# Reordering the start of an attention-plus-FFN kernel on Trainium2: first transposes of the second batch, last transposes and first values of the first

## The chip, the cores and the metric

The kernel runs on one core of one Trainium2 chip. The metric is device time in microseconds (us). Each kernel is run several times; a median and the range of its runs are quoted.

## The reference, cut to what matters

```python
scores = (1 / sqrt(64)) * q @ k.transpose(0, 1, 3, 2)   # q, k, v: 8 batches, 12 heads, 448 tokens, 64
attn   = maximum(scores, 0.0) ** 2 / 448
x      = (attn @ v), heads side by side                 # 3584 tokens x 768
g, val = x @ w_gate, x @ w_val                          # 768 -> 1536
out    = (gelu(g) * val) @ w_out                        # 1536 -> 768
```

Inputs and output are float32; the kernel computes in bf16.

## The kernel before

The host side of the kernel makes a list of pieces of work with a wished time each, sorts it, splits TensorE's work into a list for the lower and one for the upper half of the array (by `tile_position` matmuls use 64x64 quarters), and then plays the lists through a small model that decides the final order of instructions of each engine. So a change of a wished time moves instructions on all engines. Inside a batch, "transposes" turn the loaded q and k, 21 "score units" each give TensorE matmuls, one relu on ScalarE and one square on VectorE, "values" multiply the squares by v, and "gate pieces" (with w_gate or w_val) and "output pieces" (with w_out) are the FFN. The first batch has nothing to run beside its attention, so TensorE fills holes with dummy matmuls (18 with 512 columns each between 5 and 31 us in before).

```python
    def fill(t0, t1):                       # dummy matmuls in a hole of TensorE, early in the kernel only
        ...
        n = int((t1 - t0 - 0.15) / 0.22)
        if t1 > FILL or n < 1:
            return
        t = new_bank(None)
        for _ in range(n):
            nc.tensor.matmul(t[:, :], warm[:, 0:128], warm[:, :], start=True, stop=True)
...
    PLACE5 = -7.0                           # wished time of the first batch's last values
    def add_gate_value(at, b, fc, g):
        ...
        if (b, fc) == (0, 0):               # the first gate slice stands around those last values
            at = [PLACE5 - 0.5 + 0.1 * g] * 3 + [PLACE5 + 0.1] + [0.01 * g] * 2
        then(at, GS, *ops, done)
...
    for m in range(NM):                     # third batch: the last loads of the starting list
        for i in range(2):
            load_qk(2, i, 4 * m, 4 * m + 4)
    load_v(2, 0, H)
...
    LO1 = 2 * G + 2.2                       # where the second batch's attention may begin
    for b in range(B):
        if b == 0:
            lo, hi = -60.0, -12.0
        elif b == 1:
            lo, hi = LO1, starts[1] - LEAD
        ...
        step = (hi - lo) / NU
        if b < EARLY:
            for m in range(NM):
                for rs in ((0,), (1,)) if b == 0 else ((0, 1),):
                    x = (1.5 * step if rs == (1,) else -3.0) if b == 0 else -5.0 if m else -2.0
                    work.append((lo + SC * m * step + x, 1, add_transposes, (b, m, rs)))
        for pr in range(NPAIR):
            u = SC * (pr // 2) + (VC - 1, SC - 1)[pr % 2]
            x = lo + u * step + max(4.5, (3.2 if b == 0 else 2.5) * step)
            work.append((PLACE5 if (b, pr) == (0, NPAIR - 1) else x, 2, add_values, (b, pr)))
        for u in range(NU):
            work.append((lo + u * step, 3, add_scores, (b, u)))
    work.sort(key=lambda w: w[:2])
...
    def emit_warm_up():                     # the first matmuls of the program: 20 dummies
        t = new_bank(None)
        for _ in range(10):
            for j in range(2):
                nc.tensor.matmul(t[HALF[j], :], warm[:, HALF[j]], warm[:, :],
                                 start=True, stop=True, tile_position=(0, P * j))
```

## Time and profile before

| | before |
|---|---|
| time, median of the first 3 runs (range) | 428.75 us (428.64 to 429.78) |
| span of the profiled run, granted clock | 427.4 us, 0.999 |
| TensorE busy | 421.1 us, 99% |
| ScalarE, VectorE busy | 52%, 50% |
| useful TensorE work (counted as for the leads below) from 5.4 us (first transpose) to 31 us | 12.4 of 25.6 us of the array's capacity |

How to read it: TensorE is the bound, and its busy share hides two things. In the first 31 us busy time contains dummy matmuls (6.0 us from 5 to 31 us); that is where the change works. And a TensorE that stands still for some tenths of a us hardly shows, because the trace gives a 448-column matmul a length of some 0.35 us, though the next one follows 0.189 us after its start.

### The profile page before, as it was taken

The page shows a single profiled execution, that of the slowest core. Times are in us where ns is not written, and L with a number is a line of the kernel's source. Part 1 is how long each engine was busy: PE and PEld are TensorE (multiplying, and loading weights), DVE is VectorE, ACT ScalarE, POOL GpSimd, SP SyncE. Part 2 cuts the span into 40 slices and gives each one's busy share as a digit, 9 for nine tenths or more (in the row PEclk, how much of TensorE's full clock was granted, in tenths as well). Part 3 has the DMA queues.
Part 4 walks back from the last instruction along what each step waited for, and adds up shares of the span by engine and source line. Part 5 has one row for each costly group of instructions (what it writes and reads, how often), then busy time and mean ns, then how long its engine had stood idle before and what let it go on. Part 6 is the DMA issues. An engine that isn't in the chain of part 4 may idle for free.

```text
span 427.4 us, 19594 instructions
## 1 busy us (share of the span) xinstructions
PE 421.1 (99%) x9090; PEld 359.7 (84%) x9093; DVE 213.1 (50%) x347; ACT 223.5 (52%) x320; POOL 71.5 (17%) x116
## 2 busy tenths in 40 slices
PE   8999999999999999999999999999999999999996
PEld 3556768889998889889999988979999988977895
DVE  2865766367653665346643566445743555212201
ACT  4946674366655555556455565555546555322220
POOL 8655320012200131012300123011310000000000
PEclk9999999999999999999999999999999999999999
DMA  7999999978984399545965379635984100120034
GB/s 103 191 199 198 201 208 195 161 104 110 119 130 88 46 112 119 118 83 84 134 116 114 47 91 147 133 63 57 136 141 98 38 4 3 44 72 3 2 77 114
DMA packets 75217, 44.91 MB, mean 105 GB/s; under 512 B 36096, under 2 KB 71680, under 8 KB 75136
## 3 DMA queue, kind: packets, MB, share of 16 engines
q0 software_dynamic: 37088, 24.39, 42.6%
q1 hardware_dynamic: 37888, 19.08, 24.8%
q8 instruction: 71, 1.16, 1.2%
q10 hardware_dynamic: 160, 0.20, 0.1%
q14 instruction: 10, 0.08, 0.1%
HBM read 48.76 MB, written 11.01 MB: 140 GB/s over the span
## 4 chain that ended last, share of the span: by engine, by line
PE 98%; ACT 0%; issue 0%; DVE 0%; ACTq 0%
PE ff L159 86%; PE sp L159 8%; PE ff L304 1%; PE ff L699 1%; PE sp L342 1%; PE ff L342 1%; ACT rl L389 0%; DVE osb L555 0%; DVE warm L145 0%; DVE table L148 0%; ACTq L389 0%
## 5 line engine op out<-in xcount | busy, mean ns | idle before, releaser
L159 PE MATMUL ff<-xT,wg 64*64 64x448 bf16 x2304 | 218.2, 349 | 0.0
L159 PE MATMUL ff<-xT,wv 64*64 64x448 bf16 x2304 | 216.7, 349 | 0.1
L389 ACT ACTIVATE rl<-sp 128x896 bf16<-128x896 f32 x168 | 152.3, 918 | 94.3 <-PE sp L159 77.6
L159 PE MATMUL ff<-wo,uT 64*64 64x384 bf16 (+1 forms) x2736 | 151.4, 320 | 0.0
L159 PEld LDWEIGHTS <-wg 64*64 64x64 bf16 x2304 | 126.9, 107 | 17.3 <-issue 0.9
L159 PEld LDWEIGHTS <-wv 64*64 64x64 bf16 x2304 | 126.8, 107 | 17.3 <-issue 2.1
L395 DVE TENSOR_TENSOR attnT<-rl 128x896 bf16<-128x896 bf16 x168 | 103.8, 623 | 69.1 <-ACT rl L389 68.2
L159 PEld LDWEIGHTS <-uT 64*64 64x64 bf16 x2736 | 128.7, 107 | 3.9
L159 PE MATMUL sp<-qkT 64*64 64x448 bf16 (+1 forms) x768 | 108.3, 328 | 0.5 <-ACT rl L389 0.4
L503 DVE TENSOR_TENSOR uT<-gel,ff 128x448 bf16<-128x448 bf16 x96 | 59.5, 620 | 79.2 <-PE ff L159 68.4
L159 PE MATMUL ff<-attnT,v 64*64 64x448 bf16 (+1 forms) x768 | 86.2, 326 | 0.1
L498 ACT ACTIVATE gel<-ff 128x448 bf16<-128x448 f32 x96 | 52.1, 543 | 55.5 <-PE ff L159 54.7
L159 PEld LDWEIGHTS <-qkT 64*64 64x64 bf16 x768 | 44.1, 106 | 9.8 <-issue 4.2
L159 PEld LDWEIGHTS <-v 64*64 64x64 bf16 x768 | 46.7, 107 | 5.4 <-issue 1.3
L555 ACT COPY osb<-ff 128x384 f32<-128x384 f32 x54 | 25.7, 476 | 46.0 <-PE ff L159 43.3
L448 DVE TENSOR_SCALAR xT<-ff 128x448 bf16<-128x448 f32 x48 | 29.9, 623 | 31.5 <-PE ff L159 31.4
L211 POOL DMA_DIRECT2D qk<-in_q_dram x25 | 15.5, 622 | 128.7 <-DVE uT L503 121.6
L224 POOL DMA_DIRECT2D v<-in_v_dram x44 | 27.3, 627 | 41.6 <-DVE uT L503 32.0
L211 POOL DMA_DIRECT2D qk<-in_k_dram x25 | 15.4, 615 | 64.1 <-DVE uT L503 55.7
L258 DVE COPY qkr<-qk 128x1792 bf16<-128x1792 bf16 x18 | 19.3, 1077 | 0.0
L555 DVE COPY osb<-ff 128x192 f32<-128x192 f32 (+1 forms) x3 | 1.2, 421 | 18.3 <-PE ff L159 18.3
L342 PEld LDWEIGHTS <-qk 128*64 128x64 bf16 x168 | 5.5, 115 | 3.6 <-issue 3.2
(23 smaller groups left out, 44.3 us busy)
## 6 DMA issues: line engine op xcount, KB each, us to landing
out_dram<-osb SPq DMA_DIRECT2D x54, 192.0 KB, 2.9
v<-in_v_dram POOLq DMA_DIRECT2D x42, 128.0 KB, 4.0
qk<-in_q_dram POOLq DMA_DIRECT2D x23, 224.0 KB, 4.4
qk<-in_k_dram POOLq DMA_DIRECT2D x23, 224.0 KB, 4.7
wg<-in_moe_w_gate_dram POOLq DMA_DIRECT2D x6, 384.0 KB, 10.2
wv<-in_moe_w_val_dram POOLq DMA_DIRECT2D x6, 384.0 KB, 11.1
wo<-in_moe_w_out_dram POOLq DMA_DIRECT2D x4, 576.0 KB, 15.4
v<-in_v_dram POOLq DMA_DIRECT2D x2, 384.0 KB, 11.2
```

Source lines behind the costliest of these rows:

```text
L159: return nc.tensor.matmul(o, lhsT, rhs, start=start, stop=stop, tile_position=(P * row, P * col))
L211: op = load(4 * (h1 - h0) * S * D, lambda: nc.gpsimd.dma_start(tile_of().rearrange("p (h x) -> p h x", h=H)[:, h0:h1, :], src[b, h0:h1].re ...
L224: return nc.gpsimd.dma_start(v16[b][HALF[i], h0:h1, :, :], v[b, h0:h1].rearrange("h (p c) d -> p h c d", c=SC)[:, :, c0:c0 + VC, :])
L258: nc.vector.tensor_copy(qkr[b][:, m], qk16[b].rearrange("p (h c d) -> p c h d", c=SC, d=D)[:, :, 4 * m:4 * m + 4])
L304: nc.tensor.matmul(t[:, :], warm[:, 0:128], warm[:, :], start=True, stop=True)
L342: nc.tensor.transpose(t[HALF[j], c, :], src[:, 2 * (2 * m + r) + j, c, :], ident[:, :], tile_position=(0, P * j))
L389: nc.scalar.activation(rl[:, :, :], box[0][:, :, 0:S], AF.Relu)
L395: nc.vector.tensor_tensor(a[:, :, :], box[1][:, :, :], box[1][:, :, :], op=ALU.mult)
L448: nc.vector.tensor_scalar_mul(xT[b][:, pr, :], box[0][:, 0:S], scalar1=out_scale)
L498: nc.scalar.activation(gel[b, fc][:, :], box[0][:, 0:S], AF.Gelu)
L503: u_op[b, fc].ins = nc.vector.tensor_tensor(uT[b][:, fc, :], gel.pop((b, fc))[:, :], box[0][:, 0:S], op=ALU.mult).ins
L555: (nc.vector.tensor_copy if last else nc.scalar.copy)(osb[t][:, cols], box[0][:, 0:N])
```

## The change

Its intent is to use the half-empty start. The second batch's first transposes run while the first batch's last values are copied (instead of dummies and idle time), the last group's transposes of the first batch come one unit sooner, the first values come 1.5 units later, and the second batch's window starts 2.5 us sooner.

```diff
         if (b, fc) == (0, 0):
-            at = [PLACE5 - 0.5 + 0.1 * g] * 3 + [PLACE5 + 0.1] + [0.01 * g] * 2
+            at = [PLACE5 - 0.5 + 0.1 * g] * 3 + [0.01 * g] * 3
...
-    LO1 = 2 * G + 2.2
+    LO1 = 2.0
...
-                    x = (1.5 * step if rs == (1,) else -3.0) if b == 0 else -5.0 if m else -2.0
-                    work.append((lo + SC * m * step + x, 1, add_transposes, (b, m, rs)))
+                    x = -5.0 if m else -2.0
+                    if b == 0:
+                        x = (1.5 * step if rs == (1,) else -3.0) - step * (m == NM - 1)
+                    t_at = lo + SC * m * step + x
+                    if (b, m) == (1, 0):
+                        t_at = PLACE5 + 0.05
+                    work.append((t_at, 1, add_transposes, (b, m, rs)))
...
-            x = lo + u * step + max(4.5, (3.2 if b == 0 else 2.5) * step)
+            x = lo + u * step + max(4.5, (3.2 + 1.5 * (pr == 0) if b == 0 else 2.5) * step)
```

## The prediction

> **What bounds the kernel now.** First the page, for the busy shares and the chain:
>
> ```profile
> PE 421.1 (99%) x9090; PEld 359.7 (84%) x9093; DVE 213.1 (50%) x347; ACT 223.5 (52%) x320; POOL 71.5 (17%) x116
> PE 98%; ACT 0%; issue 0%; DVE 0%; ACTq 0%
> ```
>
> TensorE is 99% busy and is 98% of the chain, so nearly nothing off it can pay. But busy is not full. Matmuls here use one 64x64 quarter of the array, four run at once, and a 448-column one holds its quarter for 189 ns (starts in the trace follow at 0.189 us). Four per 0.189 us are 21.2 a microsecond. So next I counted matmuls per stretch (busy us, then count in brackets):
>
> ```profile
> 15.00:25.00 10.00, 9.36 (x146) 1.00 1.41 198
> 25.00:31.00 6.00, 5.89 (x92) 1.00 1.38 199
> 31.00:41.00 10.00, 10.00 (x218) 1.00 1.41 198
> 380.00:390.00 10.00, 10.00 (x220) 1.00 0.04 10
> ```
>
> From 31 us on the array is close to full (21.8 a us, some of them shorter pieces). Before that it runs at 15, and part of these are not work, as the groups from 5 to 31 us show:
>
> ```profile
> L304 PE MATMUL ff<-warm 128*128 128x512 bf16 x18 | 6.0, 386 | 0.3 <-issue 0.3
> ```
>
> Those are fillers[...].[...] useful work from 5.4 to 31 us is about 13 of 25.6 us. So there are some 12 us of slack at the start and almost none later; the change works in just this slack. What ends the waits there is ScalarE's list:
>
> ```profile
> 7.57 5.78 ACT L389 ACTIVATE rl<-sp 128x896 bf16<-128x896 f32 x7 [5.34 <-PE sp L159]
> 13.70 5.01 ACT L389 ACTIVATE rl<-sp 128x896 bf16<-128x896 f32 x6 [0.36 <-PE sp L159]
> 19.10 6.89 ACT L389 ACTIVATE rl<-sp 128x896 bf16<-128x896 f32 x8 [0.38 <-PE ff L159]
> ```
>
> The first batch's 21 score units are 21 relus, starting 0.797 to 0.813 us apart when nothing holds them. The first starts at 7.57, the last at 25.05: 17.48 us against 20 x 0.805 = 16.1, so about 1.4 us of it are waits for TensorE (0.47 before the 8th, 0.51 before the 14th, 0.4 in small ones). After the last relu come its square, the last values, the copies of the values (the rows of VectorE at 26.97 and 27.98) and the first gate matmuls:
>
> ```profile
> 26.93 1.00 PE L159 MATMUL ff<-attnT,v 64*64 64x448 bf16 x6
> 27.75 0.38 PE L159 MATMUL ff<-xT,wg 64*64 64x448 bf16 x2
> 28.44 0.39 PE L304 MATMUL ff<-warm 128*128 128x512 bf16 x1
> 28.76 0.38 PE L159 MATMUL ff<-xT,wg 64*64 64x448 bf16 x2
> 29.82 0.58 PE L342 MATMUL sp<-ident,qk 128*64 128x128 bf16 x14
> 30.33 0.38 PE L159 MATMUL ff<-xT,wg 64*64 64x448 bf16 x2
> 30.64 0.58 PE L342 MATMUL sp<-ident,qk 128*64 128x128 bf16 x14
> ```
>
> The last values issue at 27.37 and 27.56; their copy ends at 28.60; the gate matmul that reads it starts at 28.76. The second batch's first two transpose blocks come only at 29.82 and 30.64, one gate piece between them.
>
> [...] transposes (128x64 tiles) start 0.28 us after the preceding 64x64 piece instead of 0.189, and the next 64x64 piece starts 0.512 us after a block whose 14 matmuls issue in 0.37. A lone block thus costs about 0.8 us.[...]
>
> **The change, part by part.** No work is added or removed; TensorE's rows differ by fillers alone. I took the new order of each engine and the semaphore counts in the built program, and walked it by hand with durations from the trace: relu 0.80 from the last and 0.43 after its scores start, score after a freed buffer 0.05, transposes to copy 0.62, copies and squares 0.54 apart, fillers 0.31 plus 0.21 for each further one.
>
> (a) First values later. The 8th unit's scores now come before the first values, but four fillers instead of one stand ahead of them: 12.30 + 0.31 + 3 x 0.21 = 13.26, relu at 13.69, where it was at 13.70. No gain here.
>
> (b) Last group's transposes a unit sooner. Following the relus: 11th 16.29 (was 16.19, its transpose copy now sits behind a square), 13th 17.99 (17.78), 14th 18.80 (19.10), 16th 20.45 (20.71), 18th 22.08 (22.64), 21st 24.48 (25.05). The wait before the 14th goes, because the transposes no longer stand in front of its scores and the copy is ready in time for the 15th. VectorE is tighter in between (three more copies queue near 20 us) but ends its 21st square at 26.12 (26.645). From there the order is as before, so values, first gate pieces and last copies move by 0.57 us: the last values piece from 27.56 to 26.99. Gain 0.57.
>
> (c) The transposes while the last values are copied. Call the last values piece t. Before: next gate pieces with a 0.31 + 0.32 us hole for the copy, two lone blocks, and the first gate piece of the third slice at t + 5.71. After: block at t + 0.28, second 0.37 later with no switch between, gate at t + 0.655 + 0.512 = t + 1.17; the copy has landed by then (t + 1.04). New wait: the second batch's first scores now come three gate pieces on, and both transpose copies wait for the second block, so they are ready at t + 0.655 + 0.62 + 0.62 + 0.05 = t + 1.95, where TensorE would be at t + 1.55 to 1.73: about 0.2 us lost. Walking on, the third slice starts at t + 5.19, and each half of the array has then done one 0.189 us piece more than before. Gain 5.71 - 5.19 + 0.19 = 0.71.
>
> (d) The second batch's other transposes. Their places move as its window starts 2.5 us sooner. Second group, before (half-array idle, lower / upper): 1.80 / 1.26 us around 37.13. After: the blocks adjoin, but lone pieces stand on both sides: 1.93 / 1.37. Loss 0.12. Third group: 1.59 / 1.38 before (49.1 to 50.8), 1.73 / 1.73 after. Loss 0.25.
>
> Sum: 0.57 + 0.71 - 0.12 - 0.25 = 0.91 us. All of it is on the path, as TensorE is full from there to the end. 428.75 - 0.91 = 427.84.
>
> **The rivals.** *Loads take the wait's place.* In the stage that moves, memory delivers about 198 GB/s, and loads queue behind one another. For: a start 1 to 2 us sooner could meet weights not landed. Against: by the trace's landing events the second batch's first heads land at 23.05 and 24.18 (needed at 27.3), and the weight slices land 4.3 to 7 us before first use; the tightest is the last output weight, 64.77 against 68.12. A gain under 3 us meets none. If one did bind: no change, 428.7. *ScalarE stays the bound at the start and only gives small waits back.* If the extra fillers run longer or VectorE's queue delays the copies of transposes, (b) falls to zero and the time is 428.4. If instead all 1.4 us of relu waits went, (b) would be 1.4 and the time 427.0. *Waits in the second batch.* Its scores, relus, gelus and squares are reordered for 45 us; before has stalls of some 0.2 us there (near 42.1, 48.3, 54.6), each a buffer waited for. Three more or fewer make 428.4 or 427.3. *Pure noise:* three runs of before span 428.64 to 429.78.
>
> **Range and chances.** Centre 427.8. Error of (b) about 0.4, of (c) 0.2, of (d) and the reordering 0.4, of a median of runs 0.2; added in squares about 0.65 us, times 1.3 for 8 in 10: 426.9 to 428.7, which I widen a little at the fast side. Two per cent is 8.6 us, more than half of all slack at the start, and no wait seen can cost as much: 0.985 within 2%.
>
> **What would show it.** (a): 8th relu near 13.7, four fillers before it. (b): the idle of 0.38 before 19.10 gone, 21st relu near 24.5. (c): both transpose blocks in one run of 28 within 0.5 us of the last values, no filler after 26 us, ScalarE's first relu of the second batch near 29.9 instead of 34.03. (d): the next two transpose places as costly as before or a little more. The span after 80 us should be unchanged in shape and sooner by some 0.9 us. I am wrong if the 21st relu has not moved, if TensorE waits over 0.5 us for the transpose copies, or if stretches from 41 to 80 us hold fewer matmuls than before.

## More of the kernel before

The stretches are from the view of busy time by windows (window, its length, then busy us and instruction counts of TensorE, its weight loads, VectorE, ScalarE and GpSimd, then granted clock, DMA share and GB/s).

```profile
74.00:76.00 2.00, 2.00 (x56) 2.00 (x51) 1.15 (x2) 0.48 (x1) 0.00 (x0) 1.00 1.00 100
76.00:78.00 2.00, 2.00 (x54) 2.00 (x48) 0.47 (x1) 0.48 (x1) 0.00 (x0) 1.00 1.06 230
```

TensorE does 110 matmuls in these 4 us; nothing seems to happen here.

## The result, and the profile after

| | before | after |
|---|---|---|
| median of 6 runs each (range) | 429.06 us (428.64 to 429.78) | 428.02 us (427.75 to 429.42) |
| span of the profiled run, clock | 427.4 us, 0.999 | 426.0 us, 0.996 |

The ratio is 0.9979 with a 95% interval of 0.9963 to 0.9995: within 2%, and a little faster. The page of the changed kernel, busy shares and the chain:

```profile
PE 418.5 (98%) x9087; PEld 360.3 (85%) x9090; DVE 212.9 (50%) x347; ACT 223.7 (53%) x320; POOL 71.7 (17%) x116
PE 98%; issue 0%; ACT 0%; DVE 0%
```

TensorE's busy time fell by 2.6 us and the span by only 1.4: 1.2 us more of the span is now idle. ScalarE's list of the changed kernel (start, length, what, how many, and in brackets the idle time before it):

```profile
7.58 5.77 ACT L389 ACTIVATE rl<-sp 128x896 bf16<-128x896 f32 x7 [5.34 <-PE sp L159]
13.64 11.85 ACT L389 ACTIVATE rl<-sp 128x896 bf16<-128x896 f32 x14 [0.29 <-PE sp L159]
30.06 0.92 ACT L389 ACTIVATE rl<-sp 128x896 bf16<-128x896 f32 x1 [4.57 <-PE sp L159]
```

The runs of 6 and 8 relus have become one of 14: the wait before the 14th is gone. The second batch's first relu is at 30.06. The handover, from TensorE's timeline of the changed kernel:

```profile
26.44 1.00 PE L159 MATMUL ff<-attnT,v 64*64 64x448 bf16 x6
27.37 0.97 PE L342 MATMUL sp<-ident,qk 128*64 128x128 bf16 x28
28.28 0.75 PE L159 MATMUL ff<-xT,wg 64*64 64x448 bf16 x6
29.07 0.38 PE L159 MATMUL sp<-qkT 64*64 64x448 bf16 x2
```

One run of 28 transposes follows the last values; no dummy stands between. Then the stretches of the changed kernel:

```profile
25.00:31.00 6.00, 5.85 (x114) 3.37 (x113) 3.56 (x7) 1.41 (x2) 3.12 (x5) 1.00 1.38 199
31.00:41.00 10.00, 10.00 (x221) 7.93 (x217) 6.50 (x11) 7.18 (x10) 5.55 (x8) 1.00 1.41 198
...
74.00:76.00 2.00, 1.50 (x34) 0.98 (x26) 0.69 (x1) 0.48 (x1) 0.00 (x0) 1.00 1.48 74
76.00:78.00 2.00, 1.37 (x32) 1.24 (x35) 0.00 (x0) 0.00 (x0) 0.00 (x0) 1.00 1.11 240
```

From 25 to 31 us there are 114 matmuls, where there were 92: the change works. But from 74 to 78 us there are 66 where there were 110, with 1.13 us of idle time. The chain of waits in the stretch from 70 to 80 us says of it (start, length, what):

```profile
69.96 5.54 PE ff L159 x123
75.50 1.13 issue
76.63 3.46 PE ff L159 x63
```

"Issue" is time in which the engine waited for nothing that the profile shows: no semaphore, no buffer, no load.

To see where the time went I compared cumulative useful work. For each matmul that is not a dummy I took columns x share of the array / 2.4 columns per ns (rounded from the trace, where 448 columns in 0.189 us are 2.37 per ns), added up in order of start, and asked how much sooner the other kernel had done what before had done at a given moment. "Lead" below is that number in us:

```
us of before:            27     32     48     60     74     85    300
after               +0.49  +1.33  +1.79  +2.39  +2.55  +1.43  +1.44
```

So the start gave 0.49, the handover 0.84, the second batch gave 1.22 more up to 74 us, and 1.1 of it was lost again at the stall at 76 us.

### The profile page after: what moved, and what is told of

Same layout as the page of the kernel before. It is cut to its first block, busy times and chain, and to the rows that moved or that the text cites. A ratio compares the mean times of both kernels' runs of the same rounds, so it can differ in the third digit from the quotient of the medians. Undisturbed runs are those within 1.5% of the kernel's fastest.

```text
span 426.0 us, 19589 instructions
## 1 busy us (share of the span) xinstructions
PE 418.5 (98%) x9087; PEld 360.3 (85%) x9090; DVE 212.9 (50%) x347; ACT 223.7 (53%) x320; POOL 71.7 (17%) x116
## 3 DMA queue, kind: packets, MB, share of 16 engines
q8 instruction: 71, 1.16, 1.1%
## 4 chain that ended last, share of the span: by engine, by line
PE 98%; issue 0%; ACT 0%; DVE 0%
PE ff L159 86%; PE sp L159 8%; PE ff L705 1%; PE ff L304 1%; PE ff L342 1%; PE sp L342 1%; ACT rl L389 0%; DVE qkT L346 0%; DVE attnT L395 0%; DVE osb L555 0%; DVE warm L145 0%; DVE table L148 0%
## 5 line engine op out<-in xcount | busy, mean ns | idle before, releaser
L159 PEld LDWEIGHTS <-uT 64*64 64x64 bf16 x2736 | 126.5, 107 | 6.0 <-issue 1.6
```

The source lines that it names most:

```text
L159: return nc.tensor.matmul(o, lhsT, rhs, start=start, stop=stop, tile_position=(P * row, P * col))
```

## What stands behind the stall

The stall's matmul was mapped to its place in TensorE's program (all its instructions, counted from the kernel's first one): place 2754. Before has gaps that the prediction saw ("some 0.2 us"): the matmuls at 42.09, 48.28, 54.58 and 66.42 start 0.378, 0.394, 0.401 and 0.268 us after their forerunner, and they have places 1219, 1475, 1732 and 2244. All five places are 194 to 196 modulo 256. On the page of the changed kernel, the DMA queues (packets, MB, share) show what has this size:

```profile
q8 instruction: 71, 1.16, 1.1%
```

71 packets of 16 KB (1.16 MB / 71). TensorE has 9087 matmuls and 9090 weight loads, 18,177 in all, and 71 x 256 = 18,176. So I read each packet as one block of 256 instructions of TensorE's program, which also fits gaps that lie whole multiples of 256 places apart, to within 2. When each transfer ran, and how late TensorE went on, the traces show. Block by block (asked = moment at which a matmul just behind the last boundary started, which is an estimate of mine: in blocks 3 to 14 no transfer, in any kernel, starts more than 0.3 us before it, but later ones do by up to 1.1 us, so the real request can lie somewhat sooner):

```
                asked   transfer begins / ends    boundary passed   gap there
before, block 5    42.09     45.92 (+3.83) / 46.88       48.28       0.394
before, block 10   72.42     73.91 (+1.49) / 74.90       77.83       none
after,  block 5    40.53     43.70 (+3.17) / 44.66       46.40       none
after,  block 10   69.89     73.85 (+3.97) / 74.78       76.63       1.478
```

256 instructions take some 5.4 to 6.2 us here where nothing holds them. Waiting 3 to 4 us for the transfer to begin, 0.95 for the transfer, and some 1.3 to 1.9 after its end uses up all of that, so by this estimate a block is just in time or just late. Note block 10: its transfer begins at 73.91 in one kernel and at 73.85 in the other, although the changed kernel asks 2.5 us sooner. Up to there the loads of the starting list run, at some 200 GB/s in both kernels (198 and 197 from 70 to 72 us); the last two, the third batch's v, land at 73.87 and 75.91 in before, and at 73.24 and 77.20 in after. The kernel that asked 2.5 us sooner got its block only 0.06 us sooner.

That gives two theories for the experiments. **Instruction blocks:** TensorE stands at places near 194 modulo 256 whenever the next 16 KB block comes late, and it comes late behind the bulk loads. **Buffers** (the rival, and what the prediction said of before's gaps): these are waits for data or buffers of particular matmuls, which the reordering moved. A second question was what each part of the change gives.

## The experiments

Twelve runs were made, of ten different kernels, and all gave correct results. Leads are against the profile of before. One caution for reading them: the moment at which the first scores can start differs between profiles. The eighth relu of the first batch is at 13.70 in before and 13.69 in the kernel with the handover alone, but it ran from 13.03 to 14.31 over all, also among kernels of the same order (13.77 and 13.88, 13.28 and 13.79). So the start is read from the eighth relu on, and everything else from the growth of the lead.

```
us of before:            27     32     48     60     74     85    300
start_both          +0.84  +0.84  +1.17  +1.11  +1.17  +0.20  +0.21
hand_only           +0.02  +0.86  +0.98  +1.68  +1.79  +1.65  +1.65
after_old_window    +0.86  +1.70  +1.82  +2.52  +2.63  +2.50  +2.50
after_shift40       +0.12  +0.96  +0.60  +0.97  +0.72  +0.37  +0.37
after_v_later       +1.11  +1.94  +2.40  +3.00  +2.96  +3.11  +0.94
old_window_v_later  +0.37  +1.21  +1.33  +2.03  +2.14  +2.21  +2.21
window_only         -0.60  +0.05  +0.32  +0.92  +1.17  -0.56  -0.56
best_again          +0.25  +1.09  +1.22  +1.92  +2.02  +2.09  +1.90
old_window_again    +0.34  +1.18  +1.31  +2.01  +2.11  +1.94  +1.95
group_only          +0.99  +0.99  +1.32  +1.39  +1.16  -2.43  -2.60
values_only         +0.17  +0.18  +0.50  +1.20  +1.20  +0.64  +0.65
early_values        +0.99  +1.83  +1.96  +2.66  +2.76  +2.83  +2.83
```

### Parts of the change (first round: before 429.68 us, 428.94 to 430.48)

**start_both**: before with the two changes of the first batch.

```diff
-  x = (1.5 * step if rs == (1,) else -3.0) if b == 0 else -5.0 if m else -2.0
+  x = (1.5 * step if rs == (1,) else -3.0) - step * (m == NM - 1) if b == 0 else -5.0 if m else -2.0
...
-  x = lo + u * step + max(4.5, (3.2 if b == 0 else 2.5) * step)
+  x = lo + u * step + max(4.5, (3.2 + 1.5 * (pr == 0) if b == 0 else 2.5) * step)
```

> The kernel before with the two edits of the start alone: first values later, last group's transposes a unit sooner. The trace of the changed kernel is 0.49 us ahead in useful TensorE work when the last values of the first batch issue. Theory A (the start and the handover add up, each by itself): last values at 27.07 instead of 27.56, and about 0.5 us left at the end, ratio 0.9988. Theory B (the two edits only pay because the handover follows them): the lead at 27 us is the same 0.49, but it is gone by 32 us, ratio 1.000.

Measured: 430.23 us (428.94 to 431.39), ratio 1.0011 (0.9985 to 1.0037): the same as before. Its profile is of its fastest run. From the eighth relu to the last values piece it takes 13.42 us where before takes 13.86, so the start does gain 0.44. The lead was 1.17 until 74 us and 0.20 after: a stall of 1.04 us at place 2756 (77.71 us), where block 10's transfer began 3.89 us after it was asked for. In this profile a gain at the start was lost in one late block. Neither theory of the expectation held: the lead did not go by 32 us, and it was not there at the end.

**hand_only**: before with the handover alone, in the old window.

```diff
-            at = [PLACE5 - 0.5 + 0.1 * g] * 3 + [PLACE5 + 0.1] + [0.01 * g] * 2
+            at = [PLACE5 - 0.5 + 0.1 * g] * 3 + [0.01 * g] * 3
...
+                    if (b, m) == (1, 0):
+                        t_at = PLACE5 + 0.05
```

> The kernel before with the second batch's first transposes put while the last values are copied, the second batch's window as before. Theory A: the handover gains 0.84 us by itself (the lead of the changed kernel grew from 0.49 at 27 us to 1.33 at 32 us), last values unchanged at 27.56, ratio 0.998. Rival: without the earlier window the scores come later, so the transposes' copies are never waited for and the gain at 32 us is above 0.84, near 1.0.

Measured: 427.55 us (427.21 to 428.05), ratio 0.9950 (0.9935 to 0.9965). The lead is 0.02 before the handover and 0.86 after: the handover is worth 0.84, as theory A has it, and not the rival's 1.0. The time is better than theory A's 0.998, and by the ratios the handover alone does better than the whole change (0.9979), though the intervals just overlap (up to 0.9965, and from 0.9963). From 32 to 74 us it grows by another 0.93, though the second batch's window is the old one. In this kernel blocks wait 2.0 to 2.9 us for their transfer, where they waited 3.1 to 3.9 in before (blocks 3 to 9), and the gaps at 194 modulo 256 are gone up to block 9. One gap of 0.389 us is left at 76.25, place 2754.

**after_old_window**: the changed kernel with the second batch's old window.

```diff
-    LO1 = 2.0
+    LO1 = 2 * G + 2.2
```

> The changed kernel with the second batch's window put back by 2.5 us. It asks where the second batch's own lead of 1.2 us between 32 and 70 us came from, and what ends the stall of 1.35 us at 75.2 us. My prediction's step (d): the window costs 0.37, so this is 0.4 us faster than the changed kernel. Theory of the instruction blocks: TensorE stands still at program positions 256k+194 when the next 16 KB block of instructions comes late through loaded DMA; lead at 70 us is then set by which boundaries stall. If the lead at 70 us is only some 1.3 us here, the stall near 75 us is shorter than 0.5 us and the end is within 0.4 us of the changed kernel; if the stall belongs to the new order of the output stage, it stays at 1.3 us.

Measured: 427.65 us (426.75 to 428.15), ratio 0.9949 (0.9931 to 0.9968), so better than the change, though the intervals just overlap. The lead grows by 0.93 from 32 to 74 us, the change's by 1.22: the earlier window is worth about 0.3 there (0.2 in window_only, 1.12 against 0.93), but it costs more at block 10, where the gap is 0.353 us here and 1.478 in the change.

**after_shift40**: the changed kernel with each of the 20 dummies at the very start cut in two halves. This does the same work; it moves all later instructions of TensorE by 40 places.

```diff
-  nc.tensor.matmul(t[HALF[j], :], warm[:, HALF[j]], warm[:, :],
-                   start=True, stop=True, tile_position=(0, P * j))
+  for c in (slice(0, 256), slice(256, 512)):
+      nc.tensor.matmul(t[HALF[j], c], warm[:, HALF[j]], warm[:, c],
+                       start=True, stop=True, tile_position=(0, P * j))
```

> The changed kernel with each warm-up matmul of 512 columns cut into two of 256: same array time, 40 more rows (20 weight loads, 20 matmuls) in TensorE's program, all else the same. Theory of the instruction blocks: the stall near 75 us moves with the program position: it comes 40 rows (about 0.7 us of work) sooner, at other matmuls than now (now: the 9th upper piece of the second output half tile), again at 256k+194. Rival, a hidden semaphore wait or a bank conflict of that piece: the stall stays at the same matmul, 1.3 us long. Time within 0.7 us of the changed kernel under both.

Measured: 428.65 us (428.49 to 428.84), ratio 0.9974 (0.9957 to 0.9991). The stalls of TensorE are at places 1217, 1473, 1730, 2242 and 2754, again 193 or 194 modulo 256, but these are now other matmuls: at 76.81 us a gate piece of the second batch starts 0.684 us after its forerunner, while the output piece with the gap of 1.478 in the change has none. The chains of waits (from 38 to 50 us, then from 70 to 80 us) name nothing before the first of them, and a copy on VectorE before the last:

```profile
40.02 0.10 PE ff L159 x2
40.12 0.33 issue
...
74.44 2.08 DVE qkr L258 x2
76.52 0.29 issue
76.81 3.20 PE ff L159 x55
```

The gate piece at 76.81 does carry a wait for VectorE, so for this one gap such a wait is not excluded; but it starts 1.61 us after block 10's transfer ended (75.20), like the matmuls at the other boundaries, and 0.29 us after that copy. Over the five stalls the matmuls did not matter, their place did; this decides against buffers. It also shows that size and number of the stalls are not settled by the order alone: here blocks wait 3.4 to 4.0 us from block 4 on and four more are late, so the lead falls from 0.96 to 0.72 between 32 and 74 us.

### Loads out of the way (second round: before 429.06 us, 428.01 to 430.78)

**after_v_later**: the changed kernel, with the third batch's v loads taken from the end of the starting list and issued after the second batch's first product. They still have to land before their use.

```diff
-    load_v(2, 0, H)
...
+            if (b, fc) == (1, 0):
+                load_v(2, 0, H, [done])
```

> The changed kernel with the third batch's two loads of v (384 KB each, landing at 73.24 and 77.20 us) issued only after the second batch's first product, near 80 us; they are read near 95 us. Nothing on TensorE changes before that. Theory of the instruction blocks: the tenth block was asked for at 69.89 us and its transfer began 3.97 us later[...]; with the loads of v gone from there it begins within 2.5 us, the stall of 1.3 us at position 256k+194 shrinks below 0.4 us, and the lead over the kernel before is 2.2 us or more at 80 us instead of 1.43; ratio 0.995. Rival (the stall comes with the order of the output stage, or from the third batch's transposes by DMA, which start at 72 us): the stall stays above 1 us, ratio 0.998.

Measured: 427.94 us (427.80 to 428.29), ratio 0.9975 (0.9954 to 0.9996). Block 10 is asked for at 69.55 and its transfer begins at 71.91, so 2.36 us later instead of 3.97, and there is no stall at that block (block 9 shows a gap of 0.299 us). The windows of this kernel over the same stretch:

```profile
74.00:76.00 2.00, 2.00 (x50) 1.67 (x46) 0.35 (x1) 0.17 (x1) 0.00 (x0) 1.00 0.96 195
76.00:78.00 2.00, 2.00 (x46) 1.31 (x38) 0.00 (x1) 0.93 (x2) 0.00 (x0) 1.00 1.09 80
```

96 matmuls where the change has 66, and TensorE is busy throughout. The lead at 85 us is 3.11, and the time is still that of the change. The chain of waits from 90 to 97 us shows where it went:

```profile
79.66 13.71 DMA v<-in_v_dram
93.37 0.04 issue
93.41 1.04 PE ff L159 x18
```

The second half of v takes 13.7 us and is used at 93.41, by a matmul that starts 2.07 us after its forerunner; I had placed the load too tightly. The lead is 0.94 in the end. That the stall hangs on these loads is shown (gap at block 10: 1.478 us before they were moved, none after); the gain is not collected, and the expected ratio of 0.995 was missed for that reason.

**old_window_v_later**: the same with the old window.

```diff
-    LO1 = 2.0
+    LO1 = 2 * G + 2.2
...
-    load_v(2, 0, H)
...
+            if (b, fc) == (1, 0):
+                load_v(2, 0, H, [done])
```

> Both: the changed kernel with the second batch's window put back and the loads of v later. The old window alone had a ratio of 0.9949, a lead of 2.6 us at 74 us and a stall of only 0.35 us at 75.6 us. If the instruction block was the only thing there, little is left to gain: lead at 80 us 2.6 to 2.8 us, ratio 0.9940 to 0.9950. If the loads of v, now later, meet the stores and transposes near 80 to 90 us, some of the lead is lost there: ratio above 0.996.

Measured: 426.93 us (426.91 to 427.76), ratio 0.9955 (0.9932 to 0.9978). Block 10's transfer begins 1.01 us after it was asked for (3.13 with v in its old place), no gap at a block boundary is seen, v is in time, and the lead of 2.14 at 74 us is 2.21 at the end. Lead and ratio lie just outside of what was expected (2.6 to 2.8, and 0.9940 to 0.9950); the start of this profile came later (0.37 at 27 us, where after_old_window has 0.86).

**window_only**: before with the earlier window alone.

```diff
-    LO1 = 2 * G + 2.2
+    LO1 = 2.0
```

> The kernel before with the second batch's window 2.5 us sooner and nothing else. In the changed kernel the window made the output stage meet the loads: old window 427.65, new window 428.0 to 428.7. My step (d) read as a cost in array time: 0.37 us, ratio 1.001. If the window's harm is only that TensorE reaches the output stage sooner, before the loads are done, then here, without the lead of 1.3 us from the start, the stall at the tenth block is shorter than 1 us and the ratio is 0.999 to 1.001.

Measured: 428.38 us (427.68 to 429.73), ratio 0.9978 (0.9951 to 1.0006); the profile is of its slowest run. The lead grows by 1.12 from 32 to 74 us, and then falls by 1.73 in a stall, which the chain from 70 to 80 us shows:

```profile
69.97 7.01 PE ff L159 x159
76.98 1.48 issue
78.46 1.56 PE ff L159 x29
```

The matmul at 78.46 is at place 2754 again. Block 10's transfer ran from 74.77 to 77.07, so here the transfer itself took 2.3 us, where 0.95 is usual. The expectation said that without the lead of the start the stall would be under 1 us; it was not, so being sooner is not the window's only harm there. As this is the slowest of four runs, which spread over 2 us, the usual stall may be smaller; no other run was profiled.

### Repeats, and the two parts of the start (third round: before 429.60 us, 427.87 to 431.01)

**best_again** is old_window_v_later once more, and **old_window_again** is after_old_window once more, both in five rounds; no edit beyond those above.

> The changed kernel with the old start of the second batch's window and the third batch's v loads issued later, once more and in five rounds. If its 426.93 us was not chance, its ratio to the kernel before is 0.993 to 0.997 again, below the changed kernel's 0.9979, and its trace has no stall of TensorE at an instruction block that is over 0.2 us. If the 426.93 was chance, the ratio is 0.997 to 0.999 like the changed kernel's.

Measured: 426.91 us (426.59 to 427.24), ratio 0.9945 (0.9924 to 0.9966). Its chain from 70 to 80 us is one piece without "issue":

```profile
69.95 10.08 PE ff L159 x220
```

So the first result was not chance. The expectation of no stall held but for one of 0.265 us at 94.33, place 3522 (194 modulo 256), which is just above the 0.2 that was set: block 13's transfer began 3.86 us after it was asked for. The moved loads may still have run then (in after_v_later the second one did until 93.37), but this was not traced here.

> The changed kernel with only the old start of the second batch's window, once more and in five rounds. Theory: this window is worth some 0.5 to 1 us less stall at the tenth instruction block, so the ratio is 0.994 to 0.997 and the stall near 75.5 us is under 0.7 us. Rival: the size of that stall is chance from run to run, whatever the window, and this profile may then show over 1 us and a ratio like the changed kernel's, 0.998.

Measured: 427.15 us (427.07 to 427.76), ratio 0.9952 (0.9930 to 0.9975). The gap at place 2754 is 0.390 us, after 0.353 in the first profile of the same order. So the smaller stall with the old window repeats, and the rival of chance falls as far as two profiles tell.

**group_only**: before with the last group's transposes sooner, and **values_only**: before with the first values later. Each is one of the two edits of start_both, run once for its trace.

> The kernel before with the last group's transposes one unit sooner and nothing else. If the prediction's step (b) is right and independent of step (a), the last values come about 0.57 us sooner relative to the first relu (the time from the first relu to the last values piece 19.99 us before, about 19.4 here) and the gap before the 14th relu goes. If the gain needs the first values later too, the time stays within 0.2 us of 19.99. Stalls of TensorE, if any, lie at positions 194 modulo 256.

Measured: one run of 431.82 us. The part at the start does what it should. The rows of ScalarE from the eighth relu on show no wait before the 14th:

```profile
13.44 11.56 ACT L389 ACTIVATE rl<-sp 128x896 bf16<-128x896 f32 x14 [0.36 <-PE sp L159]
```

The last values piece comes 19.58 us after the first relu (19.99 in before; about 19.4 was expected) and 13.13 after the eighth (13.86). The lead is 0.99. Then TensorE stalls at five boundaries, all at 193 or 194 modulo 256. The chain from 70 to 82 us shows the largest:

```profile
71.42 5.59 PE ff L159 x122
77.01 1.98 issue
78.99 3.02 PE ff L159 x38
```

Block 10 was asked for at 71.42, and its transfer began only at 76.30, 4.88 us later. The lead falls from 1.16 to -2.43, which is more than the stall. The windows after it show the rest (the number after the five engines is the granted clock):

```profile
80.00:81.00 1.00, 1.00 (x16) 0.54 (x9) 0.00 (x0) 0.48 (x1) 0.00 (x0) 0.59 1.34 299
81.00:82.00 1.00, 1.00 (x14) 0.67 (x13) 0.00 (x0) 0.54 (x1) 0.00 (x0) 0.50 1.79 120
```

The clock is granted at 0.59, 0.50, 0.50 and 0.71 in the four us from 80 to 84, which by an estimate, with work in proportion to the clock, costs 4 - 2.30 = 1.7 us (70 matmuls in these 4 us, 28 in each of the two us after them at 1.00); with some 2.1 us of stall (2.303 between two starts, where some 0.19 is usual) that is 3.8, against 3.59 of lead lost. The pause of 2.07 us in after_v_later was not followed by such a drop (its clock is 1.00 from 93 to 100 us). What lowered the clock here, no run shows.

> The kernel before with the first values later and nothing else. Step (a) says no gain: the time from the first relu to the last values piece stays 19.8 to 20.1 us (19.99 before). The rival is that the first values in front of the eighth unit's scores were what held the eighth relu: then it is 19.5 to 19.6 us.

Measured: one run of 428.56 us. From the first relu to the last values piece it takes 20.14 us, a little more than expected, and 14.08 from the eighth relu, so 0.22 more than before. The rows of ScalarE:

```profile
13.31 5.07 ACT L389 ACTIVATE rl<-sp 128x896 bf16<-128x896 f32 x6 [0.29 <-PE sp L159]
18.93 6.89 ACT L389 ACTIVATE rl<-sp 128x896 bf16<-128x896 f32 x8 [0.55 <-PE ff L159]
```

The wait before the 14th relu is 0.55 where it was 0.38. The eighth relu comes 6.06 us after the first, where it came after 6.13. So the first values later gain 0.07 and lose 0.22.

### The part that loses taken back (fourth round: before 429.33 us, 428.53 to 429.89)

**early_values**: the best kernel so far (old window, v later) with the first values in their old place.

```diff
-  x = lo + u * step + max(4.5, (3.2 + 1.5 * (pr == 0) if b == 0 else 2.5) * step)
+  x = lo + u * step + max(4.5, (3.2 if b == 0 else 2.5) * step)
```

> The best kernel so far (changed kernel, old window of the second batch, third batch's v loads later; 426.91 us, ratio 0.9945) with the first values back at their old place. Counted from the eighth relu of the first batch, the last values piece came 13.86 us later in the kernel before, 13.43 with both changes of the start, 13.13 with the last group sooner alone and 14.08 with the values later alone. If these two are independent of the rest, it is 13.1 to 13.2 us here, and the time is 0.2 to 0.4 us below the best kernel's: 426.5 to 426.8, ratio 0.993 to 0.995. Rival: the shifted program position brings a late instruction block back, as in every kernel whose start was altered alone; then stalls of TensorE at positions 194 modulo 256 give the time 427 to 428.5.

Measured: 426.37 us (426.09 to 427.01), ratio 0.9940 (0.9927 to 0.9954). From the eighth relu to the last values piece it takes 13.13 us, to the hundredth what group_only has; the time is just below the expected 426.5 to 426.8. Blocks 3 to 9 wait 2.3 to 3.0 us and block 10 waits 1.5; no gap at a boundary shows, and the chain from 70 to 80 us is one piece:

```profile
69.99 10.02 PE ff L159 x209
```

This kernel is the fastest: its slowest run (427.01) is below the fastest of the change (427.75) and of before (427.87 over all rounds). The intervals of its ratio and of the change's (0.9963 to 0.9995) do not touch. Against the kernel best_again it is 0.5 us faster by the medians, but these are of different rounds and the intervals of the ratios overlap.

## Why the prediction was right

The time was predicted at 427.8 us and came out at 428.02, and 1.04 us of gain by the medians stands against 0.91 predicted. The sum was right; not every term was, and part of it was luck, as (d) shows. The walk by hand took TensorE's matmuls in the order of the program, so that one that waits holds all behind it; that was the assumption, and no run tests it alone. (The prediction's 13 us of useful work from 5.4 to 31 us is 12.4 by recount; no term rests on it.)

**(a), no gain from the first values later.** The eighth relu is at 13.64 (13.69 predicted; 12.30 + 0.31 + 3 x 0.21 is 13.24 and not 13.26, which would make it 13.67), as it should be. But values_only shows a loss of 0.22 us after it, which the walk had not given to this part: the wait before the 14th relu grows (0.55 us, 0.38 in before) when the last group's transposes keep their place.

**(b), 0.57 us from the transposes sooner.** Together with (a) it measured 0.50 in the pair of profiles (last values piece at 27.07 instead of 27.56, first relus at 7.58 and 7.57), and 0.42 to 0.44 from the eighth relu on in all eight profiles with both edits against the three with neither. Alone it is worth 0.73. The idle time before the 14th is gone as predicted, and the 21st relu is at 24.55 (24.48 predicted, 25.05 before). The mechanism was right, and the size 0.1 too high.

**(c), 0.71 us from the handover.** With t the last values piece, at 27.066: gate piece at t + 1.21 (t + 1.17 predicted), first scores at t + 2.00 (t + 1.95), with the small wait for the transposes' copies that was foreseen: the scores start 0.388 us after the piece before them, instead of 0.189. The third slice is at t + 5.06 (t + 5.19). The gain is 5.71 - 5.06 + 0.19 = 0.84, and the lead grows by 0.83 or 0.84 from 27 to 32 us in all nine profiles with the handover, with either window. The earlier window alone gives 0.65 there (window_only), so the two overlap. The switch times of 0.28 and 0.512 us, which the prediction read from the trace, carried it.

**(d), a loss of 0.37 us in the second batch.** This step failed in its mechanism, and up to 74 us in its sign. From 32 to 74 us the lead grew by 1.22. Some 0.93 of that is not of the window at all: it comes in hand_only and after_old_window too, and values_only, with neither handover nor window, has 1.02; these are kernels in which the blocks of instructions come in time up to 74 us. The four gaps of before hold about 0.7 of it (1.44 less 4 x 0.19); the rest was not traced. What remains for the window is +0.2 to +0.3. That the change without the window is faster after all (by 0.4 us in the medians, which are of different rounds) comes from block 10 and not from array time. Half-array idle times around the second and third groups of transposes were real pieces of the trace, but they were not what set the time there.

**The rivals.** "Loads take the wait's place" was turned down because the weights land early enough: the gate and value slices 4.3 us or more before their use, the last output weight 3.35. (In before, the four loads of output weights, issued from 41.7 to 46.1 us, landed 14.4 to 18.7 us later.) The changed kernel shows no wait for a weight at the stall; the loads took the wait's place through the instruction blocks: block 10's transfer began 3.97 us after it was asked for, and 2.36 with v's loads moved. "Waits in the second batch" named before's gaps near 42.1, 48.3 and 54.6, "each a buffer waited for". That was wrong: after_shift40 shows that they follow the place in the program. The sum came out by luck, because two errors of this kind nearly cancelled: +1.2 before 74 us and -1.1 at block 10, so about +0.1 for the whole second batch where the prediction has -0.37. Its own test, "stretches from 41 to 80 us hold fewer matmuls than before", did fire for 74 to 78 us.

**What stays open.** Under the same bulk loads of some 200 GB/s, blocks 4 to 9 wait 2.0 to 3.3 us for their transfer in hand_only, window_only, early_values and the kernels with handover and old window, 2.8 to 3.6 in the change and after_v_later, and 3.1 to 4.0 in before, start_both, group_only, values_only and after_shift40. I do not know what decides this. With fewer loads queued the wait at block 10 was shorter (2.36 us in after_v_later instead of 3.97), but no run shows how a block waits among the loads. Over blocks 3 to 14 of all kernels a transfer began up to 4.9 us after the last boundary was passed, and TensorE went on no sooner than 1.3 us after its end; the transfer took 0.89 to 1.09 us in blocks 3 to 10 of before and after, up to 1.9 in blocks 11 to 14 of before, and 2.3 at most (window_only). Where 194 comes from is open as well; 62 instructions ahead of the kernel's first would give it (256 - 194, an estimate), and none is recorded. The variation of the first scores between profiles was not studied.

## What to carry to other kernels

When an engine that bounds a kernel stands still and the profile names nothing that it waits for, count its place in the program: here TensorE's gaps had a constant remainder modulo 256 (193 to 196), and that led to instruction blocks that came late (gaps of 0.265 to 2.303 us between starts). The changed kernel asked for block 10 2.5 us sooner and got it 0.06 us sooner, in a stage with loads of some 200 GB/s, so 1.1 us of a gain won at the start were lost at one boundary; loads that are not needed yet can be issued later, with their own use checked (block 10's wait fell from 3.97 to 2.36 us). And run each part of a change alone: here one part lost 0.2 us inside a sum that gained, and without it, with the old window and with the loads moved, the kernel came to 426.37 us.
